# Weight conversions, unit steps and weight requests of a fused attention and mixer kernel moved in their order

## Chip, cores and metric

The kernel runs on one core of one Trainium2 chip. The metric is device time of one execution in microseconds. The core has five engines with queues of their own: TensorE (PE, matrix products), VectorE (DVE), ScalarE (ACT), GpSimd (POOL) and SyncE (SP, which here issues most transfers). Each runs its instructions in a fixed order and waits, at an instruction, until what that needs is done.

## The reference

Three stages follow one another for 4 sequences of 448 tokens, in float32: causal attention of 12 heads of 64, a mixer (tokens, then channels), and a second mixer with rotations.

```
scores = q @ k.T / 8, causal mask; attn = softmax(scores); x = attn @ v   # 4 x 12 heads, 448 x 64
u  = x + (relu(x.T @ w_tok1) @ w_tok2).T          # 448 -> 256 -> 448 tokens
x  = u + relu(u @ w_ch1) @ w_ch2                  # 768 -> 1536 -> 768 channels
theta = x @ w_theta
y  = w_tok_r @ (x * cos(theta)) + w_tok_i @ (x * sin(theta))
u  = x + y
out = u + relu(u @ w_ch)
```

The weights arrive as float64.

## The kernel before

**Pairs and steps.** Attention runs over 24 pairs of heads (6 in each sequence), each in 7 tiles of queries: 168 *steps*. A step's scores are one product on PE (line 273, for pairs from the ninth on with a second product at 275 for the low part of k). DVE masks them and finds the row maximum (L280), ACT takes the exponential (L282). For the first twelve pairs PE then transposes the result (L289), ACT copies it (L291) and PE multiplies it with v (L317). From the 13th pair on ACT writes a 16-bit high part `ph` (L110), DVE a low part (L302), SP issues a DMA that transposes both (`pt`, L305), and PE multiplies with v split in three (L328; DVE makes the splits `v_mid`). The product with v comes four steps behind its score (`LAG`). After every second pair `tokmix` does the token mixer for these heads.

**Units.** The channel mixer is cut into 96 *units*, 24 for each sequence: 12 weight tiles of `w_ch1` (`ch1_unit`) and 12 of `w_ch2` (`ch2_unit`), each 18 products on PE (L169 to L171: values and weights are split in a high and a low part) with one weight tile of 768 KB in `ws`, and one or two sums on ACT and DVE (L385, L386, L394). Units of a sequence that is done run between the steps of the next ones. `UNIT_STEPS` says at which step each runs: the first at step 46, 18 in the first 42 steps, then 26 in every 42. Units that are left run behind the last step.

**Conversions.** A weight tile is fetched as raw 64-bit words (L123), made float32 by one operation of ACT (L126) and four of DVE (L133 to L137), and split by ACT (L110) and DVE (L117) into `ws`. All 24 tiles of the channel mixer are converted during attention, and stored for the later sequences (`w_c<-ws`, L445). `ROUND_STEPS` says at which step each conversion starts: the first four are the token mixer's, four tiles of the channel mixer (`EARLY`) at steps 20 to 38 are stored and read again for the first sequence's units (L164), the other 20 start five steps ahead of their unit, which takes the tile directly from the conversion. `ws` has four buffers.

**Requests.** `run_units` asks, ahead of each unit, for the weight tiles of this and the next two units (`load_unit`), if they are stored. SP issues all of these transfers, in order, with the loads of q, k and v and the transposes.

**Order.** Within this the order of each engine's instructions is set when the program is built, by a scheduler with priorities (scores, their products with v and the loads of pairs come first) and a model of its own. So a table of steps also moves instructions that it doesn't name.

Of the kernel before, what the change touches and what calls it, by code (L numbers as in the profile page):

```python
# [21 lines left out]
NPR = H // 2  # L22
# [9 lines left out]
AHEAD, LAG, LOOK = 500, 4, 2  # L32
KEEP, UBACK = 6, 16
LATE_CONVERT = 16
FIRST_UNIT, PHASE, RATES = 46, 42, (18, 26)
EARLY = 4
UNIT_STEPS = [FIRST_UNIT + -(-n * PHASE // RATES[0]) if n < RATES[0] else
              FIRST_UNIT + PHASE + -(-(n - RATES[0]) * PHASE // RATES[1]) for n in range(72)]
ROUND_STEPS = [3, 4, 8, 9] + [20, 26, 32, 38] + [UNIT_STEPS[n] - 5 for n in range(EARLY, 24)]
ENGINES = {  # L40
    0: dict(qhi="A", qlo="D", khi="A", klo="D", v="D", phi="A", xhi="A", xlo="D", uhi="A", ulo="D"),
}
# [10 lines left out]
def fused(ctx, tc, q, k, v, w_tok1, w_tok2, w_ch1, w_ch2, w_theta, w_tok, w_ch, out):  # L53
# [15 lines left out]
    nc = tc.nc  # L69
# [29 lines left out]
    def hl_tile(tag):  # L99
        return main.tile([P, 2, S], F32R, tag=tag, name=tag, bufs=BUFS[tag])  # L100
# [4 lines left out]
    def f32v(ap):  # L105
        return ap.bitcast(F32)

    def copy_to(eng, dst, src, scale=1.0):
        if eng == "A":
            nc.scalar.activation(dst, src, AF.Copy, scale=scale)  # L110
        else:
            e = nc.gpsimd if eng == "P" else nc.vector
            e.tensor_scalar(out=dst, in0=src, scalar1=scale, scalar2=0.0, op0=ALU.mult, op1=ALU.add)  # L113

    def rest_to(eng, dst, src, hi):
        e = nc.gpsimd if eng == "P" else nc.vector
        e.tensor_tensor(out=dst, in0=src, in1=f32v(hi) if hi.dtype == F32R else hi, op=ALU.subtract)  # L117

    def raw_tile():
        return cv.tile([P, E, 2], U32, tag="raw", name="raw", bufs=BUFS["raw"])  # L120

    def fetch64(src, raw):
        nc.sync.dma_start(out=raw[:, :src.shape[-1]].rearrange("p n w -> p (n w)"), in_=src.bitcast(U32))  # L123
# [18 lines left out]
    def split_w(dst, f):  # L142
        copy_to("A", dst[:, 0], f)
        rest_to("D", dst[:, 1], f, dst[:, 0])
# [6 lines left out]
    def ws_tile():  # L151
        return main.tile([P, 2, E], F32R, tag="ws", name="ws", bufs=BUFS["ws"])
# [9 lines left out]
    def stream_tile(kept):  # L162
        w = ws_tile()
        nc.sync.dma_start(out=f32v(w), in_=kept)  # L164
        return w
# [29 lines left out]
    def tok_weights(n):  # L195
        if n < 2:
            cols = slice(n * 512, (n + 1) * 512)
            return w_tok1[:, cols], wt1[:, :, cols]
        return w_tok2[:, (n - 2) * S:(n - 1) * S], wt2[:, n - 2]
# [9 lines left out]
    def prep(b, pr):  # L209
        qr = ap2.tile([P, 2 * S], F32, tag="qk_raw", name="q_raw", bufs=2)  # L210
        if b * NPR + pr in NATIVE:
            kr = ap2.tile([P, 2 * S], F32, tag="kh", name="k_pad")
            for t, src in ((kr, k), (qr, q)):
                (nc.vector if b * NPR + pr == 0 and t is kr else nc.gpsimd).memset(t[64:128], 0.0)
                if b * NPR + pr == 0 and t is qr:
                    for c in (slice(0, 2 * P), slice(2 * P, 2 * S)):
                        nc.scalar.dma_start(out=t[0:64, c], in_=src[b, pr, 0:64, c])
                else:
                    loads[b * NPR + pr] = nc.sync.dma_start(out=t[0:64], in_=src[b, pr, 0:64])
        else:  # L220
            loads[b * NPR + pr] = nc.sync.dma_start(out=qr, in_=q[b, pr])
            kr = ap2.tile([P, 2 * S], F32, tag="qk_raw", name="k_raw", bufs=2)
            nc.sync.dma_start(out=kr, in_=k[b, pr])
        vr = ap2.tile([P, 9 * D], F32, tag="v_raw", name="v_raw")
        nc.sync.dma_start(out=vr, in_=v[b, pr])
        if b * NPR + pr in NATIVE:
            qs, kh, kl = qr, kr, None
        else:
            qs = ap2.tile([P, 2 * S], F32R, tag="qs", name="qs")
            copy_to(pick("qhi"), qs, qr)  # L230
            rest_to(pick("qlo"), qs[64:128], qr[64:128], qs[64:128])
            kh = ap2.tile([P, 2 * S], F32R, tag="kh", name="kh")
            copy_to(pick("khi"), kh, kr)
            kl = ap2.tile([P, 2 * S], F32R, tag="kl", name="kl")
            rest_to(pick("klo"), kl, kr, kh)
        if b * NPR + pr in NATPV:
            return qs, kh, kl, (vr,)
        v1 = vr.bitcast(BF16).rearrange("p (n w) -> p n w", w=2)[:, :, 1]
        vm = ap2.tile([P, 9 * D], F32, tag="v_mid", name="v_mid", bufs=1)
        rest_to(pick("v"), vm, vr, v1)  # L240
        v2, v3 = (vm.bitcast(BF16).rearrange("p (n w) -> p n w", w=2)[:, :, z] for z in (1, 0))
        rest_to(pick("v"), v3, vm, v2)
        return qs, kh, kl, (v1, v2, v3)
# [157 lines left out]
    loaded = {}  # L401

    jobs = [((w_ch1, w_ch2)[c - 1][fh * 6 + t], wd[f"c{c}", fh, t]) for _, fh, c, t in units[:24]]
    late = [(w_ch[e], wd["c3", 0, e]) for e in range(DT)]

    def load_unit(n):
        if n < len(units) and n not in loaded and (n >= 24 or n in stored):
            b, fh, c, t = units[n]
            loaded[n] = stream_tile(wd[f"c{c}", fh, t])

    fetched, rounding, stored = {}, {}, set()
    at, halves = [0], [0]

    def split_ready():

        while halves[0] < B * DT:
            b, d = divmod(halves[0], DT)
            if accs[b][d] is None or (d >= BUFS["ut"] - DT and at[0] < 24 * (b - 1) + 18):
                return
            t = hl_tile("ut")  # L420
            copy_to(pick("uhi"), t[:, 0], accs[b][d])
            rest_to(pick("ulo"), t[:, 1], accs[b][d], t[:, 0])
            uTs[b][d] = t
            halves[0] += 1

    def fetch(j):
        if j < len(ROUND_STEPS):
            src = tok_weights(j)[0] if j < 4 else jobs[j - 4][0]
            fetched[j] = src, raw_tile()
            fetch64(*fetched[j])  # L430

# [3 lines left out]
        abs64(rounding[j], raw)  # L435

    def round_rest(j):
        f = rounding.pop(j)
        round64(f, fetched.pop(j)[1])
        if j < 4:  # L440
            split_w(tok_weights(j)[1], f)
        else:
            w, kept = ws_tile(), jobs[j - 4][1]
            split_w(w, f)
            nc.sync.dma_start(out=kept, in_=f32v(w))  # L445
            stored.add(j - 4)
            if j - 4 >= EARLY:
                loaded[j - 4] = w
        fetch(j + 2)

    made = [0]
# [7 lines left out]
    def run_units(n):  # L459
        for _ in range(n):  # L460
            u = at[0]
            for ahead in range(LOOK + 1):
                load_unit(u + ahead)
            b, fh, c, t = units[u]
            if c == 1:
                ch1_unit(b, uTs[b], fh, t, loaded[u])
            else:
                ch2_unit(b, uTs[b], accs[b], fh, t, loaded[u])
            loaded[u] = None
            at[0] += 1  # L470
            split_ready()


# [2 lines left out]
    def pick(what):  # L476
        turn[what] = turn.get(what, -1) + 1
        return eng[what][turn[what] % len(eng[what])]
# [17 lines left out]
    for n, (b, pr, t) in enumerate(steps):  # L496
        if t == 0:
            eng.update(ENGINES.get(b * NPR + pr, {}))
        if t == 0:
            pairs[b, pr] = Pair(b, pr, parts[b, pr])  # L500
        with tc.high_priority(AHEAD):
            scores(pairs[b, pr], *TILES[t])
        if n == 0:
            fetch(0)
            fetch(1)
        for j, at_step in enumerate(ROUND_STEPS):
            if at_step == n - 1:
                with tc.issue_after(pairs[b, pr].first.ins):
                    round_rest(j)
            if at_step == n:  # L510
                with tc.issue_after(pairs[b, pr].last.ins):
                    round_first(j)
        if n >= 140:
            convert_late((n - 136) // 4)
        if t == 0 and (b, pr) != (B - 1, NPR - 1):
            nx = (b + (pr + 1) // NPR, (pr + 1) % NPR)
            with tc.high_priority(AHEAD), ExitStack() as es:
                if nx == (0, 1):
                    es.enter_context(tc.issue_after(loads[0].ins))
                parts[nx] = prep(*nx)  # L520
        if n >= LAG:
            with tc.high_priority(AHEAD):
                late_step(n - LAG)
        if n == FIRST_UNIT - 4:
            load_unit(0)
            load_unit(1)
        run_units(sum(at_step == n for at_step in UNIT_STEPS))
    for n in range(len(steps) - LAG, len(steps)):
        late_step(n)
# [111 lines left out]
    for b in range(B):  # L641
        raw, x2 = [], []
        for d in range(DT):
            r = acc_tile()
            nc.sync.dma_start(out=r, in_=x2d[b][d])
            t = hl_tile("ut")
# [126 lines left out]
```

## Time and profile before

| | us |
|---|---|
| three timed runs | 936.09, 937.81, 940.9 |
| median | 937.81 |
| profiled execution | 935.52 |
| its span, first to last instruction | 933.7 |
| PE busy | 903.5 |
| DVE busy | 633.0 |

The profile is one execution. A span's time counts from its first instruction. A wait is put down to what came last by the record; where several things are waited for, the one named may not be the one that held. L and a number is the line of the kernel.

### The profile page before, as it was taken

The numbers are of one execution on the slowest core, as the hardware profiler recorded it, in microseconds if no ns is written. First come the engines' busy times: TensorE is split into PE (matmuls) and PEld (weight loads), VectorE is DVE, ScalarE is ACT, GpSimd is POOL, SyncE is SP. The second block draws the span as 40 slices with busy tenths as digits, with TensorE's granted clock in tenths as the row PEclk, the third lists the DMA queues.
The fourth block names the chain that finished last, engine by engine and source line by source line (L and its number), as shares of the span: only waits on it lengthen the run. The fifth ranks groups of instructions, "written<-read, shape, count | busy, mean of one in ns | idle before, by whom it ended". The sixth has DMA issues, their size and how long they took to land.

```text
span 933.7 us, 15879 instructions
## 1 busy us (share of the span) xinstructions
PE 903.5 (97%) x5820; PEld 827.0 (89%) x5820; DVE 633.0 (68%) x1467; ACT 389.5 (42%) x914; POOL 109.5 (12%) x178
## 2 busy tenths in 40 slices
PE   7999999999879999999999999999999999999998
PEld 5888898988758899989989899999999999999997
DVE  5687798989997667667873398745764467475351
ACT  5777667667655545544632234312211202112100
POOL 2110000000000000000000000022531143242120
PEclk9999999999999999999999999999999999999999
DMA  5475686869899999699798599764605135153043
GB/s 169 133 248 197 235 288 206 293 225 262 246 285 318 323 250 238 227 263 279 232 315 260 178 352 401 261 207 134 200 1 152 56 114 166 29 161 109 24 131 127
DMA packets 103677, 193.65 MB, mean 207 GB/s; under 512 B 60784, under 2 KB 72880, under 8 KB 103600
## 3 DMA queue, kind: packets, MB, share of 16 engines
q1 hardware_dynamic: 102288, 190.84, 65.0%
q0 software_dynamic: 1152, 1.57, 0.9%
q8 instruction: 46, 0.75, 0.3%
q10 hardware_dynamic: 160, 0.23, 0.1%
q14 instruction: 31, 0.25, 0.1%
HBM read 143.85 MB, written 34.60 MB: 191 GB/s over the span
## 4 chain that ended last, share of the span: by engine, by line
PE 75%; DMA 12%; DVE 8%; ACT 3%; issue 2%; POOL 0%; SPq 0%; ACTq 0%; POOLq 0%; DVEq 0%
PE ps_mm L169 17%; PE ps_mm L170 17%; PE ps_mm L171 17%; DMA pt<-ph 7%; PE ps_sc L273 3%; PE ps_pv L317 3%; PE ps_sc L170 3%; PE ps_sc L169 3%; PE ps_sc L171 3%; PE ps_pv L328 2%; DMA ws<-w_c 2%; PE ps_mm L289 2%; DMA raw<-in_w_ch_dram 1%; DMA q_raw<-in_q_dram 1%; PE ps_sc L275 1%
## 5 line engine op out<-in xcount | busy, mean ns | idle before, releaser
L171 PE MATMUL ps_mm<-h,ws 128*128 128x448 f32 x432 | 159.7, 370 | 1.0 <-DVE ws L117 1.0
L169 PE MATMUL ps_mm<-h,ws 128*128 128x448 f32 x432 | 159.9, 370 | 0.5 <-ACT ws L110 0.5
L170 PE MATMUL ps_mm<-h,ws 128*128 128x448 f32 x432 | 159.7, 370 | 0.0
L169 PE MATMUL ps_mm<-ut,ws 128*128 128x448 f32 x288 | 106.8, 371 | 1.7 <-DMA ws<-w_c 1.7
L170 PE MATMUL ps_mm<-ut,ws 128*128 128x448 f32 x288 | 105.9, 368 | 0.0
L171 PE MATMUL ps_mm<-ut,ws 128*128 128x448 f32 x288 | 105.7, 367 | 0.0
L282 ACT ACTIVATE sb<-sb,mx 128x192 f32<-128x192 f32 (+3 forms) x168 | 89.5, 534 | 38.9 <-DVE mx L280 38.4
L171 PEld LDWEIGHTS ps_mm<-h,ws 128*128 128x128 f32 x432 | 81.6, 189 | 8.8 <-DVE ws L117 1.7
L169 PEld LDWEIGHTS ps_mm<-h,ws 128*128 128x128 f32 x432 | 81.5, 189 | 8.1 <-ACT ws L110 0.7
L170 PEld LDWEIGHTS ps_mm<-h,ws 128*128 128x128 f32 x432 | 81.6, 189 | 6.9
L280 DVE CUSTOM_DVE_ANT_0 sb<-ps_sc,mask 128x192 f32<-128x192 f32 (+3 forms) x168 | 74.6, 454 | 15.2 <-PE ps_mm L289 11.1
L113 POOL TENSOR_SCALAR ut<-acc 128x448 fp32r<-128x448 f32 x24 | 17.2, 722 | 508.4 <-PE ps_mm L355 450.0
L577 ACT ACTIVATE tmp<-ps_sc 128x384 f32<-128x384 f32 x28 | 13.5, 483 | 132.2 <-PE ps_sc L171 132.1
L317 PEld LDWEIGHTS ps_pv<-v_raw,ptf 128*128 128x128 f32 x456 | 58.7, 191 | 6.3 <-ACT ptf L291 2.2
L317 PE MATMUL ps_pv<-v_raw,ptf 128*128 128x128 f32 (+1 forms) x456 | 62.6, 275 | 1.3 <-issue 0.6
L302 DVE SCALAR_TENSOR_TENSOR ph<-sb,ph 128x64 f16<-128x64 f32 (+3 forms) x156 | 42.9, 316 | 27.3 <-ACT ph L110 26.7
L169 PEld LDWEIGHTS ps_mm<-ut,ws 128*128 128x128 f32 x288 | 54.1, 188 | 6.1 <-DMA ws<-w_c 1.9
L110 ACT ACTIVATE ph<-sb 128x192 f16<-128x192 f32 (+3 forms) x84 | 36.8, 444 | 53.4 <-DMA pt<-ph 52.9
L170 PEld LDWEIGHTS ps_mm<-ut,ws 128*128 128x128 f32 x288 | 54.2, 188 | 4.4 <-issue 0.2
L171 PEld LDWEIGHTS ps_mm<-ut,ws 128*128 128x128 f32 x288 | 54.1, 188 | 4.2
L386 DVE SCALAR_TENSOR_TENSOR h<-ps_mm,h 128x448 fp32r<-128x448 f32 x48 | 29.7, 618 | 34.2 <-ACT h L385 34.0
L584 ACT ACTIVATE tmp<-tmp 128x384 f32<-128x384 f32 x28 | 14.7, 526 | 85.5 <-DVE tmp L582 85.5
(151 smaller groups left out, 2110.1 us busy)
## 6 DMA issues: line engine op xcount, KB each, us to landing
ws<-w_c SPq DMA_DIRECT2D x100, 768.0 KB, 5.7
raw<-in_w_ch_dram SPq DMA_DIRECT2D x30, 768.0 KB, 5.1
w_c<-ws SPq DMA_DIRECT2D x30, 768.0 KB, 4.7
q_raw<-in_q_dram SPq DMA_DIRECT2D x16, 448.0 KB, 4.2
k_raw<-in_k_dram SPq DMA_DIRECT2D x16, 448.0 KB, 4.7
v_raw<-in_v_dram SPq DMA_DIRECT2D x24, 288.0 KB, 4.1
x2d<-acc SPq DMA_DIRECT2D x24, 224.0 KB, 4.7
acc<-x2d SPq DMA_DIRECT2D x24, 224.0 KB, 3.2
```

The source lines that it names most:

```text
L110: nc.scalar.activation(dst, src, AF.Copy, scale=scale)
L169: nc.tensor.matmul(ps, lhsT=ka(a[:, 0]), rhs=kb(b[:, 0]), start=first, stop=False)
L170: nc.tensor.matmul(ps, lhsT=ka(a[:, 0]), rhs=kb(b[:, 1]), start=False, stop=False)
L171: nc.tensor.matmul(ps, lhsT=ka(a[:, 1]), rhs=kb(b[:, 0]), start=False, stop=last)
L273: nc.tensor.matmul(ps[:, 0:n], lhsT=lhs, rhs=cut(pp.kh), start=True, stop=pp.kl is None)
L280: pp.first = nc.vector.tensor_tensor_reduce(out=dst, in0=src, in1=msk, op0=ALU.add, op1=ALU.min, scale=-0.125, scalar=3.0e38, accum_out=pp ...
L282: pp.last = nc.scalar.activation(sb[:, 0:kk], sb[:, 0:kk], AF.Exp, bias=pp.mx[:, j:j + 1], scale=-1.0, accum_out=pp.sm[:, j:j + 1])
L289: nc.tensor.transpose(pst[:, u * P:(u + 1) * P], full[:, c0 + u * P:c0 + (u + 1) * P], ident)
L302: nc.vector.scalar_tensor_tensor(out=dst, in0=sb[:, c0:c1], scalar=PSC, in1=hi[:, c0:c1], op0=ALU.mult, op1=ALU.subtract)
L317: nc.tensor.matmul(pp.ps[:, reg:reg + n], lhsT=pt[:, u], rhs=pp.v[0][:, vt * D:vt * D + n], start=(u == 0), stop=(u == len(blks) - 1))
L328: nc.tensor.matmul(pp.ps[:, reg:reg + D], lhsT=pt[:, blk], rhs=pp.v[c][:, vt * D:(vt + 1) * D], start=(n == 0), stop=(n == len(jobs) - 1))
L386: gates[0] = nc.vector.scalar_tensor_tensor(out=t[:, 1], in0=ps[:, 0:S], scalar=0.0, in1=f32v(t[:, 0]), op0=ALU.max, op1=ALU.subtract)
```

## The change

`UNIT_STEPS` gets other rates: 14 units in the first 42 steps from 46 on, then 29 in every 42. The conversions get a table of their own: six tiles (0 to 5) four steps apart from step 18 on and five more (14, 16, 18, 20, 22) between steps 43 and 70 are converted ahead, stored, and read again; the other 13 start five steps ahead of their unit and are taken directly. Requests for weight tiles stand behind a unit: for the next two units for the first 24, for the next three after that. The clearing of the lower half of the first q tile goes from POOL to DVE.

```diff
-FIRST_UNIT, PHASE, RATES = 46, 42, (18, 26)
-EARLY = 4
+FIRST_UNIT, PHASE, RATES = 46, 42, (14, 29)
-ROUND_STEPS = [3, 4, 8, 9] + [20, 26, 32, 38] + [UNIT_STEPS[n] - 5 for n in range(EARLY, 24)]
+AHEAD_STEPS = {0: 18, 1: 22, 2: 26, 3: 30, 4: 34, 5: 38, 14: 43, 16: 47, 18: 51, 20: 55, 22: 70}
+ROUNDINGS = sorted([(at_step, n - 4) for n, at_step in enumerate((3, 4, 8, 9))] +
+                   [(AHEAD_STEPS.get(n, UNIT_STEPS[n] - 5), n) for n in range(24)])
...
-                (nc.vector if b * NPR + pr == 0 and t is kr else nc.gpsimd).memset(t[64:128], 0.0)
+                (nc.vector if b * NPR + pr == 0 else nc.gpsimd).memset(t[64:128], 0.0)
...
     def fetch(j):
-        if j < len(ROUND_STEPS):
-            src = tok_weights(j)[0] if j < 4 else jobs[j - 4][0]
+        if j < len(ROUNDINGS):
+            n = ROUNDINGS[j][1]
+            src = tok_weights(n + 4)[0] if n < 0 else jobs[n][0]
...
     def round_rest(j):
-        f = rounding.pop(j)
+        n, f = ROUNDINGS[j][1], rounding.pop(j)
         round64(f, fetched.pop(j)[1])
...
             nc.sync.dma_start(out=kept, in_=f32v(w))
-            stored.add(j - 4)
-            if j - 4 >= EARLY:
-                loaded[j - 4] = w
+            stored.add(n)
+            if n not in AHEAD_STEPS:
+                loaded[n] = w
...
             u = at[0]
-            for ahead in range(LOOK + 1):
-                load_unit(u + ahead)
+            load_unit(u)
...
             at[0] += 1
+            for ahead in range(LOOK + (u >= 24)):
+                load_unit(at[0] + ahead)
             split_ready()
```

In the changed program's rows line numbers are one to three higher behind the table.

POOL's order at the start of the program, before (`k_pad` and `q_raw` are the padded tiles of a pair's k and q, `sb` and `x` work tiles):

```order
L214 MEMSET k_pad 64x896
L178 MEMSET mask 128x448
masks.py:199 ISA
masks.py:199 AFFINE_SELECT ident<-ident 128x128
L191 MEMSET sb_148 128x64
L191 MEMSET sb_150 128x64
L191 MEMSET sb_152 128x64
L204 MEMSET x_154 128x128
L204 MEMSET x_156 128x128
L214 MEMSET q_raw 64x896 x2
L179 AFFINE_SELECT mask<-mask 128x128
```

and now:

```order
L215 MEMSET k_pad 64x896
L215 MEMSET q_raw 64x896
L179 MEMSET mask 128x448
masks.py:199 ISA
masks.py:199 AFFINE_SELECT ident<-ident 128x128
L192 MEMSET sb_148 128x64
L192 MEMSET sb_150 128x64
L192 MEMSET sb_152 128x64
L205 MEMSET x_154 128x128
L205 MEMSET x_156 128x128
L180 AFFINE_SELECT mask<-mask 128x128
```

Of the two clearings of `q_raw` that stood next to each other behind the work tiles, the first pair's has gone to DVE and the second pair's stands ahead of them.

DVE's order from the 96th score on, before (`ws` and `wf` are a conversion's tiles, `x` attention's result, L372 and L394 sums of tokmix and of a unit):

```order
L280 ISA sb_152,mx<-ps_sc,mask 128x320
L280 ISA mx 128x1
L117 TENSOR_TENSOR v_mid<-v_raw 128x576
L335 TENSOR_TENSOR x_154<-ps_pv,sm 128x384
L340 TENSOR_SCALAR x_154<-ps_pv,sm 64x64 x2
L117 TENSOR_TENSOR ws<-wf,ws 128x768
L137 SCALAR_TENSOR_TENSOR wf<-raw,wf 128x768
L280 ISA sb_148,mx<-ps_sc,mask 128x448
L280 ISA mx 128x1
L372 TENSOR_TENSOR acc<-ps_mm,acc 128x448 x2
L302 SCALAR_TENSOR_TENSOR ph<-sb_150,ph 128x64
L302 SCALAR_TENSOR_TENSOR ph<-sb_150,ph 128x256
```

and now:

```order
L281 ISA sb_152,mx<-ps_sc,mask 128x320
L281 ISA mx 128x1
L118 TENSOR_TENSOR v_mid<-v_raw 128x576
L336 TENSOR_TENSOR x_154<-ps_pv,sm 128x384
L341 TENSOR_SCALAR x_154<-ps_pv,sm 64x64 x2
L281 ISA sb_148,mx<-ps_sc,mask 128x448
L281 ISA mx 128x1
L118 TENSOR_TENSOR kl<-k_raw,kh 128x896
L281 ISA sb_150,mx<-ps_sc,mask 128x448
L281 ISA mx 128x1
L118 TENSOR_TENSOR qs<-q_raw,qs 64x896
L134 TENSOR_SCALAR wf<-wf 128x768
```

The two conversion operations between the 96th and the 97th score are gone from there, and the 98th score follows one operation behind the 97th.

SP's order around the first transposes, before (`raw` is a conversion's fetch, `w_c<-ws` its store, the numbers in `w_c` the tile):

```order
L223 DMA k_raw<-in_k_dram 128x896
L445 DMA w_c_1_4_103<-ws 128x1536
L305 DMA_TRANSPOSE pt<-ph 128x2x128
L123 DMA raw<-in_w_ch_dram 128x1536
L305 DMA_TRANSPOSE pt<-ph 128x3x128
L445 DMA w_c_1_5_104<-ws 128x1536
L225 DMA v_raw<-in_v_dram 128x576
L305 DMA_TRANSPOSE pt<-ph 128x3x128
L305 DMA_TRANSPOSE pt<-ph 128x5x128
```

and now:

```order
L224 DMA k_raw<-in_k_dram 128x896
L124 DMA raw<-in_w_ch_dram 128x1536
L165 DMA ws<-w_c_1_2_101 128x1536
L447 DMA w_c_1_1_100<-ws 128x1536
L306 DMA_TRANSPOSE pt<-ph 128x2x128
L306 DMA_TRANSPOSE pt<-ph 128x3x128 x2
L124 DMA raw<-in_w_ch_dram 128x1536
L165 DMA ws<-w_c_1_4_103 128x1536
L226 DMA v_raw<-in_v_dram 128x576
```

Two weight tiles of the first sequence (14 and 16) are now read back here, where before the conversions' stores and a fetch stood between the transposes.

## Rows read from the trace of the kernel before

**Rows 1.** Part 1 of the page: busy us (share of the span) and instructions.
```profile
PE 903.5 (97%) x5820; PEld 827.0 (89%) x5820; DVE 633.0 (68%) x1467; ACT 389.5 (42%) x914; POOL 109.5 (12%) x178
```

**Rows 2.** Busy time by stretch: length, PE, PEld, DVE, ACT, POOL, clock, DMA, GB/s.
```profile
0.00:77.30 77.30, 70.54 (x470) 60.02 (x471) 54.55 (x163) 54.29 (x151) 12.96 (x27) 1.00 0.57 172
77.30:204.50 127.20, 125.20 (x819) 115.35 (x818) 105.18 (x231) 85.74 (x196) 1.98 (x2) 1.00 0.72 250
204.50:307.50 103.00, 89.66 (x737) 80.80 (x736) 94.16 (x234) 64.18 (x150) 0.00 (x0) 0.98 0.94 282
307.50:470.90 163.40, 161.70 (x1346) 146.93 (x1344) 114.26 (x318) 83.24 (x204) 0.00 (x0) 1.00 0.91 256
...
528.00:933.70 405.70, 401.14 (x2073) 373.31 (x2071) 238.52 (x467) 85.29 (x182) 94.54 (x150) 1.00 0.47 154
```

**Rows 3.** The same view: 26 us within the third stretch, and 20 of products alone.
```profile
256.00:282.00 26.00, 19.32 (x184) 16.02 (x182) 25.46 (x66) 15.05 (x38) 0.00 (x0) 0.93 0.95 269
...
560.00:580.00 20.00, 20.00 (x101) 18.46 (x100) 15.86 (x40) 8.77 (x21) 0.83 (x1) 1.00 1.03 407
```

**Rows 4.** Waits of PE, 204.5 to 307.5: us in total, times, longest.
```profile
PE ps_pv L328 <- DMA pt<-ph: 8.6, 6, 2.1
PE ps_mm L169 <- DMA ws<-w_c: 1.7, 1, 1.7
PE ps_pv L328 <- issue: 1.2, 1, 1.2
```

**Rows 5.** DVE's groups, 204.5 to 307.5: busy us, mean ns, idle before.
```profile
L137 DVE SCALAR_TENSOR_TENSOR wf<-raw,wf 128x768 uint32<-128x768 uint32 x9 | 8.6, 954 | 0.0
L136 DVE SCALAR_TENSOR_TENSOR wf<-raw,wf 128x768 uint32<-128x768 uint32 x9 | 8.6, 953 | 0.0
L117 DVE TENSOR_TENSOR ws<-wf,ws 128x768 fp32r<-128x768 f32 x8 | 7.7, 958 | 0.1
...
L133 DVE TENSOR_SCALAR wf<-wf 128x768 f32<-128x768 f32 x9 | 5.0, 556 | 0.8 <-ACT wf L126 0.8
L134 DVE TENSOR_SCALAR wf<-wf 128x768 uint32<-128x768 uint32 x9 | 5.0, 555 | 0.0
...
L386 DVE SCALAR_TENSOR_TENSOR h<-ps_mm,h 128x448 fp32r<-128x448 f32 x7 | 4.3, 621 | 0.6 <-ACT h L385 0.6
...
L394 DVE TENSOR_TENSOR acc<-ps_mm,acc 128x448 f32<-128x448 f32 x6 | 3.7, 611 | 0.0
L302 DVE SCALAR_TENSOR_TENSOR ph<-sb,ph 128x256 f16<-128x256 f32 x8 | 3.4, 423 | 0.0
...
L117 DVE TENSOR_TENSOR v_mid<-v_mid 128x576 bf16<-128x576 f32 x4 | 3.3, 831 | 0.0
```

**Rows 6.** Instructions in order of time, the first 6 us: start, us, what.
```profile
0.76 1.46 SPq L219 DMA_DIRECT2D k_pad<-in_k_dram  x2
...
3.32 1.63 POOL L214 MEMSET q_raw<- 64x896 f32 x2
...
5.07 1.41 PE L273 MATMUL ps_sc<-k_pad,q_raw 128*128 128x128 f32 x4 [5.07 <-POOL q_raw L214]
```

**Rows 7.** Transfers issued in the first 0.9 us: KB each, us to landing.
```profile
k_pad<-in_k_dram SPq DMA_DIRECT2D x1, 224.0 KB, 4.2
```

**Rows 8.** Transfers issued from 204.5 to 307.5; last, tiles in ws alone.
```profile
ws<-w_c SPq DMA_DIRECT2D x6, 768.0 KB, 6.9
...
pt<-ph SPq DMA_TRANSPOSE x28, 4.8
...
DMA to landing us min/median/max: 3.2/6.0/9.5
```

**Rows 9.** Waits of SP, 204.5 to 307.5: us in total, times, longest.
```profile
SPq L305 <- DVE ph L302: 10.8, 10, 2.7
...
SPq L445 <- DVE ws L117: 5.4, 3, 3.7
```

More of the change, by code (lines that the diff above doesn't have):

```diff
@@ L437, in round_rest @@
     def round_rest(j):
-        f = rounding.pop(j)
+        n, f = ROUNDINGS[j][1], rounding.pop(j)
         round64(f, fetched.pop(j)[1])
-        if j < 4:
-            split_w(tok_weights(j)[1], f)
+        if n < 0:
+            split_w(tok_weights(n + 4)[1], f)
         else:
-            w, kept = ws_tile(), jobs[j - 4][1]
+            w, kept = ws_tile(), jobs[n][1]
             split_w(w, f)
             nc.sync.dma_start(out=kept, in_=f32v(w))
-            stored.add(j - 4)
-            if j - 4 >= EARLY:
-                loaded[j - 4] = w
+            stored.add(n)
+            if n not in AHEAD_STEPS:
+                loaded[n] = w
         fetch(j + 2)
@@ L505, in fused @@
             fetch(1)
-        for j, at_step in enumerate(ROUND_STEPS):
+        for j, (at_step, _) in enumerate(ROUNDINGS):
             if at_step == n - 1:
```

## Prediction

> **What bounds the kernel now.** I started from the busy shares of the whole execution. TensorE (PE) is busy 903.5 of 933.7 us, VectorE (DVE) 633.0 [rows 1]. So nothing but about 30 us of PE idle time, and what hides inside busy time, can be won by any reordering, for the matrix products are the same before and after. Then I read busy time by stretch, cut at PE's 43rd, 85th and 117th score product (scores of a step: one of 168) [rows 2]. The reader is to see where the idle time sits. From 77.3 to 204.5 us PE is busy 125.20 of 127.20. From 204.5 to 307.5 it is busy 89.66 of 103.00: 13.3 us idle, more than in any other stretch. In this one stretch DVE is busy 94.16 us, 91%; in the 26 us from 256 it is 25.46, 98%, with PE at 19.32 [rows 2, 3]. From 307.5 on PE is again busy 161.70 of 163.40.
>
> The waits in that stretch name DMA: PE's second product of attention waits 8.6 us in six waits for transposed probabilities (pt) [rows 4]. But a transpose lands in 4.8 us at the median [rows 8], and SyncE (SP), which issues it, waits itself: 10.8 us in ten waits for DVE's low part of the probabilities [rows 9]. So the chain is score, DVE, ScalarE, DVE, SP, DMA, PE, and the engine that is full in it is DVE. What fills DVE is above all five operations for each converted weight tile, 954, 953, 958, 556 and 555 ns, 3.98 us a tile [rows 5], some nine times in this stretch, 35 us of the 94.
>
> One more place: PE starts at 5.07 us behind GpSimd's (POOL) clearing of q_raw, issued at 3.32 for 1.63 [rows 6]. The same score waits for k_pad, whose transfer is issued at 0.76 and lands 4.2 us later, at 4.96 [rows 6, 7].
>
> **The change part by part.** *Clearing q_raw on DVE.* POOL's end at 4.95 goes, k_pad's landing at 4.96 stays. Gain 0.0 to 0.1 us; I take 0. DVE's extra clearing stands ahead of its first score and is hidden: DVE has 54.55 us of work in 77.3 [rows 2].
>
> *Conversions.* Counted in the order of the two programs between DVE's 85th and 117th score, the DVE operations of conversions go from 42 to 34: one fewer at each of lines 133 and 134, two fewer at 136, 137 and 117 (ws). That is 0.556 + 0.555 + 2 x 0.953 + 2 x 0.954 + 2 x 0.958 = 6.8 us [rows 5]. Against it stand one more operation at each of lines 386 and 394 (0.62 + 0.61) and one more v_mid split with two fewer at line 302 (0.83 less 2 x 0.42, nothing). DVE's load in the stretch becomes 94.2 - 6.8 + 1.2 = 88.6 us. The work comes back ahead of score 43: nine operations more, 2 x 0.556 + 2 x 0.555 + 0.953 + 2 x 0.954 + 2 x 0.958 = 7.0 us, on 54.55 of 77.3, so DVE stands at 80% there. PE waited 6.8 us there with 54.55, most of it the start; I price what may be added with the tighter stretch below.
>
> *Units, 14 and 10.* A unit is 18 products. A stretch of such products has 101 in 20.00 us, 0.198 us each [rows 3]. Between PE's 43rd and 85th score the unit products go from 253 to 207, -46; up to the 117th from 233 to 260, +27; behind it +19. In stretches where PE is full this is time: -9.1 us from 77.3 to 204.5, +3.8 us behind 307.5. In between 27 x 0.198 = 5.3 us of PE work go into a stretch that has 13.3 us of holes. This is the main term: DVE sets that stretch's length, and PE's work in it is free up to the holes.
>
> *How long that stretch is then.* From PE: 89.66 + 5.3 = 95.0 us of busy time. From DVE: 88.6 us; at the share of now (91%) that is 97 us, at the 97% of its first 77.5 us 92. The upper end is that the holes stay: 103.0 + 5.3 = 108.3. The lower end is PE full, and the clock too: the granted clock of the 26 us from 256 is 0.93, so 3.6 us at 1.2 GHz instead of 2.4, after PE had been idle in the waits for pt [rows 3, 4]; that cost 1.8 us, and 95.0 - 1.8 = 93.2. I take 97, where the nearest row, DVE's share of the same stretch, puts it, and PE's own bound lies 2 us below.
>
> Weight loads are busy 80.80 us in this stretch, and 18.46 of 20.00 where PE is full [rows 2, 3]. The Trainium skill (Perfetto Trace Analysis, "Identifying the Most-Contended Engine") says that matmul busy time is no good measure of how near TensorE is to its limit, and that the busy share of weight loads is; by that rule the stretch holds 80.80 / 0.923 = 87.5 us of work in place of 89.66, 92.8 with the new units, and the lower end would be 0.4 us lower. The trace leans to it, since the half clock stands in matmul busy time.
>
> *The tighter stretch before.* From 77.3 to 204.5 DVE keeps nearly its load (105.18 less 2.8 by the same counting: three unit operations, and little of the conversions) while the stretch loses 9.1 us: 87% of 118 us instead of 83%. It also has one heap: between DVE's 77th and 78th score now stand two tiles' worth of conversions and the sums of tokmix, some 14 us. There PE can wait. Bounds: nothing, or the share of idle time that the full stretch shows now, 13% of some 35 us, 4.5 us. I take 2 us for this and the start together.
>
> *Weights that come back from memory.* Eleven instead of four tiles of the first batch are stored and read again. Reads in the stretch land in 6.9 us at the median [rows 8]. They are asked for behind a unit for the unit after next, some 2.9 steps of 3.2 us (103.0 / 32), 9.3 us ahead. Covered at the median; 0 now, the worst is a rival. For units from the 25th on the new place of the request names the same three tiles one unit boundary earlier, 0.
>
> *Sum.* Stretch 77.3 to 204.5: -9.1. Stretch to 307.5: 103.0 to 97, -6.0. Behind: +3.8. New waits: +2. Together -9.3 us. The profiled execution took 935.52 us (span 933.7); so 926.2 in its terms. The three timed runs have a median of 937.81 (936.09 to 940.9), 2.3 above the profiled one; on their scale 928.5.
>
> **The rivals.** *Holes filled, clock kept.* PE becomes the bound of the stretch, 93.2 us, and no new wait comes: -9.1 - 9.8 + 3.8 = -15.1, 922.7. For it: DVE's 88.6 us lie below PE's 93. Against: from a score to the landing of its transpose is a chain of five hand-overs, and DVE's order is fixed in heaps.
>
> *The holes only move.* The heap ahead of DVE's 78th score and the fuller stretch before it cost as much as the full stretch gives back. Four and a half us there, 2 at the start, and a stretch of 100 in place of 97 give -9.1 - 3.0 + 3.8 + 6.5 = -1.8, 936. For it: eight of 42 conversion operations is a small relief. Against: PE idled only 2.0 us at 83% DVE [rows 2].
>
> *Late weights, slower.* In the stretch the DMA engines are 94% busy [rows 2]; SP is held by a store up to 3.7 us [rows 9], and the slowest tile took 9.5 to land [rows 8], 13.2 together against 9.3 of notice. Then a reloaded unit stops PE for up to 3.9 us, and the scores queued behind it on PE too. The five tiles 14, 16, 18, 20 and 22 alone make 5 x 3.9 = 19.5 us, -9.3 + 19.5 = +10, 948. It decides from a mean lateness of 1.9 us on. Against: six such reads in this stretch now cost PE one wait of 1.7 us [rows 4, 8], and conversions fetch fewer raw tiles there.
>
> **How the numbers follow.** Forecast 928.5, with 0.50, its own range 923 to 934 (2 us of each of the two uncertain terms, the stretch's 97 and the new waits' 2, and a run's spread of 2). Filled holes 0.17 at 922.7; moved holes 0.20 at 936; late weights 0.13 at 948. The range reaches to the moved holes with a run's spread, 940, and down to 919, and leaves out the late weights and little else. About 0.5%, 4.7 us, is what a measurement of this kernel can tell from no change: faster is below 933.1. That holds for the filled holes, for 0.47 of the forecast's 0.50 and for 0.01 of the moved ones: 0.65. Within: 0.03, 0.18 of the moved and 0.02 of the late weights: 0.23. Slower: 0.12.
>
> **What would show it.** Right: the stretch from PE's 85th to 117th score lasts 95 to 99 us, PE busy over 96% of it, DVE near 88 us; the 85th score comes near 195 us, the 117th near 292; PE's wait for transposed probabilities falls from 8.6 us to under 4; PE still starts at 5.0. Wrong: the 85th score comes later than 200 us (heap before it), the stretch lasts over 103 us (DVE's chain is not the bound), or PE waits for weight reads more than 4 us in all (late weights). A start before 4.5 us would show that k_pad did not hold PE.

## The result, and the profile after

The changed kernel took 928.39 us (median of four runs, 925.48 to 930.39), the kernel before, on the same chip, 936.95 (the three timed runs and a fourth of 935.7): a ratio of 0.989, with a 95% interval of 0.9867 to 0.9913. The forecast was 928.5.

The profiled execution took 928.29 us with a span of 926.5, against 935.52 and 933.7. First part 1 of the page: busy us, share of the span, instructions.

```profile
PE 903.3 (97%) x5820; PEld 828.8 (89%) x5820; DVE 633.5 (68%) x1468; ACT 387.5 (42%) x914; POOL 108.6 (12%) x177
```

PE is busy as long as before, 903.3 against 903.5 us [rows 1]. So of the 7.2 us by which the span is shorter 7.0 are idle time of PE: 30.2 us before, 23.2 now. Where it went is in the busy time by stretch, cut at the same scores as in [rows 2] (the 43rd falls at 76.7 us, the 85th at 196.1, the 117th at 293.0):

```profile
0.00:76.70 76.70, 69.60 (x469) 59.61 (x470) 60.93 (x170) 56.85 (x152) 12.44 (x26) 1.00 0.62 196
76.70:196.10 119.40, 116.25 (x770) 108.85 (x769) 104.57 (x231) 85.60 (x199) 1.62 (x2) 0.99 0.82 290
196.10:293.00 96.90, 94.26 (x764) 86.70 (x763) 88.48 (x224) 58.53 (x139) 0.00 (x0) 0.96 0.99 291
293.00:926.50 633.50, 623.19 (x3826) 573.65 (x3822) 379.50 (x845) 186.55 (x426) 94.58 (x150) 1.00 0.62 191
```

The third row is the one to read. PE idled 13.3 us of this stretch before and now idles 2.6; it is busy 97% of the stretch. The four stretches changed by -0.6, -7.8, -6.1 and +7.3 us. Next, all waits of PE over the whole span (us in total, times, longest):

```profile
PE ps_sc L274 <- DMA k_pad<-in_k_dram: 5.0, 1, 5.0
PE ps_mm L354 <- ACT xg L111: 2.6, 2, 1.8
PE ps_pv L329 <- DMA pt<-ph: 2.3, 3, 1.3
PE ps_sc L274 <- DVE mx L281: 1.9, 4, 0.6
PE ps_mm L355 <- DVE xg L118: 1.9, 1, 1.9
PE ps_pv L329 <- issue: 1.9, 1, 1.9
...
PE ps_mm L170 <- DMA ws<-w_c: 0.4, 1, 0.4
```

The 8.6 us for `pt` of [rows 4] are 2.3 now; the 1.7 for weights read back are 0.4. DVE's conversion operations between 196.1 and 293.0 us, to be laid beside [rows 5] (busy us, mean ns, idle before):

```profile
L138 DVE SCALAR_TENSOR_TENSOR wf<-raw,wf 128x768 uint32<-128x768 uint32 x8 | 7.7, 958 | 0.1
L137 DVE SCALAR_TENSOR_TENSOR wf<-raw,wf 128x768 uint32<-128x768 uint32 x8 | 7.6, 954 | 0.0
L118 DVE TENSOR_TENSOR ws<-wf,ws 128x768 fp32r<-128x768 f32 x6 | 5.7, 957 | 0.3 <-ACT ws L111 0.2
...
L134 DVE TENSOR_SCALAR wf<-wf 128x768 f32<-128x768 f32 x7 | 3.9, 558 | 0.0
L135 DVE TENSOR_SCALAR wf<-wf 128x768 uint32<-128x768 uint32 x7 | 3.9, 552 | 0.0
```

28.8 us in place of the 34.9 that [rows 5] add up to: 6.1 us gone, of the same durations. And the transfers issued in this stretch, with the median us to landing, to be laid beside [rows 8]:

```profile
ws<-w_c SPq DMA_DIRECT2D x10, 768.0 KB, 7.3
...
pt<-ph SPq DMA_TRANSPOSE x27, 5.1
```

Both are a little slower than before (6.9 and 4.8), and PE waits for neither as it did. So the time that a transpose takes was not what PE's old waits were about. That it came late because its input did is tested by light_before below.

### The profile page after: what moved, and what is told of

Read it like the earlier page. It is cut to its first block, busy times and chain, and to the rows that moved or that the text cites. A ratio compares the mean times of both kernels' runs of the same rounds, so it can differ in the third digit from the quotient of the medians.

```text
span 926.5 us, 15932 instructions
## 1 busy us (share of the span) xinstructions
PE 903.3 (97%) x5820; PEld 828.8 (89%) x5820; DVE 633.5 (68%) x1468; ACT 387.5 (42%) x914; POOL 108.6 (12%) x177
## 4 chain that ended last, share of the span: by engine, by line
PE 80%; DMA 10%; DVE 5%; ACT 3%; issue 1%; SPq 1%; ACTq 0%; DVEq 0%
PE ps_mm L172 17%; PE ps_mm L170 17%; PE ps_mm L171 17%; DMA pt<-ph 9%; PE ps_pv L318 4%; PE ps_sc L274 3%; PE ps_sc L172 3%; PE ps_sc L170 3%; PE ps_sc L171 3%; PE ps_mm L290 2%; PE ps_pv L329 2%; PE ps_mm L354 1%; PE ps_mm L355 1%; PE ps_mm L356 1%; DMA raw<-in_w_tok_dram 1%
## 5 line engine op out<-in xcount | busy, mean ns | idle before, releaser
L386 ACT ACTIVATE h<-ps_mm 128x448 fp32r<-128x448 f32 x48 | 25.9, 539 | 59.9 <-PE ps_mm L172 59.9
## 6 DMA issues: line engine op xcount, KB each, us to landing
v_raw<-in_v_dram SPq DMA_DIRECT2D x24, 288.0 KB, 4.9
```

Of the source, the lines that this page charges most:

```text
L386: nc.scalar.activation(t[:, 0], ps[:, 0:S], AF.Relu)
```

## The experiments

The theory was the prediction's: DVE's load sets the length of the dense stretch (85th to 117th score), and the change gains what PE had idled there. Medians below stand beside a median of the kernel before on the same chip.

**The new unit rates alone.** The kernel before with one line changed:

```diff
-FIRST_UNIT, PHASE, RATES = 46, 42, (18, 26)
+FIRST_UNIT, PHASE, RATES = 46, 42, (14, 29)
```

> The kernel before with the unit rates 14 and 29 and nothing else; its conversions stay five steps ahead of their units, so they slide into the dense stretch with them. Counted in the order of this program between the 85th and 117th score: 60 DVE operations of conversions in place of 42 (47.7 us in place of 33.7), 196 unit products in place of 233; 53 products fewer ahead of it, 90 more behind. Theory (DVE's load sets this stretch): DVE has 94.2 + 14.0 = 108 us there, the stretch lasts 108 to 113 us although PE has 7.3 us less to do in it; in all -10.5 + 8 + 17.8 = +15, about 952 us. Rival (the later units make the gain, the table of conversions is of no account): 928 to 932 us. Rival (SP's transposes set the stretch): with 7.3 us less PE work in it about 101 to 103 us, +7, 944 us.

Measured: 949.26 us (945.18 to 953.82) beside 936.93, ratio 1.0117 (1.0089 to 1.0145). Busy time by stretch:

```profile
191.00:240.00 49.00, 45.55 (x359) 41.71 (x358) 47.86 (x117) 34.36 (x78) 0.00 (x0) 0.97 0.86 258
240.00:300.00 60.00, 44.10 (x296) 37.98 (x296) 51.40 (x121) 29.56 (x64) 0.00 (x0) 0.80 0.93 248
```

The total is what the theory gave within 3 us. The first rival is out; the second's 944 lies only 1.2 us below the fastest run, and light_before decides on it. The place was misjudged, by the theory's 108 to 113 us and by the second rival's 101 to 103: by PE's scores the stretch lasts 97.0 us, since PE issued its 117th score at 288.0 and went on with units and tokmix until DVE took the score up, 27 us later, with 14 more operations of conversions ahead of it; by DVE's own scores it is 196.8 to 315.2, 118 us. In the first row DVE is busy 98%, in both together PE idles 19.4 us of 109. PE's waits from 191 to 300 us show the links of the chain that [rows 4] and [rows 9] had shown:

```profile
PE ps_pv L328 <- DMA pt<-ph: 7.3, 3, 4.0
PE ps_sc L273 <- DVE mx L280: 4.9, 4, 1.9
PE ps_mm L169 <- ACT ws L110: 3.0, 2, 2.4
...
```

**The table of conversions alone.** The changed kernel with the old rates:

```diff
-FIRST_UNIT, PHASE, RATES = 46, 42, (14, 29)
+FIRST_UNIT, PHASE, RATES = 46, 42, (18, 26)
```

> The changed kernel with the old unit rates 18 and 26: only the table of conversions, the requests and the clearing are new. Between the 85th and 117th score 26 DVE operations of conversions in place of 42 (20.8 us in place of 33.7) and, as the order comes out, 291 unit products in place of 233; 6 products more ahead, 64 fewer behind. Theory (DVE's load sets the stretch): DVE has about 84 us there, PE 89.7 + 58 x 0.198 = 101 us and is the bound, the stretch lasts 101 to 104 us; +1.2 + 0 - 12.7 + 2 of waits ahead, where DVE has 6 us more: about 927 us (924 to 931), the whole gain without the new rates. Rival (the rates make the gain): 935 to 938 us. Rival (heaps ahead of the 85th score cost what is won): the 85th score comes after 209 us, 935 us or more.

Measured: 929.12 us (927.33 to 932.53) beside 936.93, ratio 0.9913 (0.9886 to 0.9939). The stretches from the 43rd, from the 85th and from the 117th score:

```profile
76.80:204.80 128.00, 125.81 (x824) 116.81 (x823) 113.33 (x242) 89.70 (x204) 1.53 (x2) 1.00 0.87 307
204.80:307.70 102.90, 100.06 (x794) 90.72 (x793) 83.49 (x219) 59.17 (x145) 0.00 (x0) 0.98 0.94 277
307.70:927.00 619.30, 605.04 (x3743) 557.49 (x3738) 376.94 (x837) 182.90 (x417) 95.09 (x150) 1.00 0.61 188
```

This has the gain of the whole change without the rates, as far as the two intervals tell (0.9867 to 0.9913 for the change). The dense stretch is as long as before, but PE is busy 100.06 us of it in place of 89.66: 291 unit products stand in it, 58 more, and 64 fewer behind. The scheduler pulled the units forward as soon as DVE left room. Not all of it arrives: behind the 117th score PE has 13.1 us less to do than before, but idles 14.3 us there in place of 8.1. And DVE at 89% from 76.8 to 204.8 us costs PE only 2.2 us there.

**DVE's load taken out of the kernel before.** In the last nine conversions three of four operations are skipped:

```diff
-        nc.vector.tensor_scalar(out=f, in0=f, scalar1=W64_MIN, ...
+        if not light:
+            nc.vector.tensor_scalar(out=f, in0=f, scalar1=W64_MIN, ...
...
-        round64(f, fetched.pop(j)[1])
+        round64(f, fetched.pop(j)[1], j - 4 >= 15)
```

> The kernel before, but the conversions of the last nine tiles (those that start from step 76 on) leave out three of their four DVE operations behind ScalarE's (lines 133, 134 and 136; the tiles' values are then not the weights): 2.07 us less DVE work a tile, 18.6 us in all. The order follows: between the 85th and 117th score 21 conversion operations in place of 42, 311 unit products in place of 233, 77 fewer behind. Theory (DVE's load sets the stretch): PE's idle time in it falls from 13.3 us to under 4, PE is busy over 96% of it, and the total falls by 9 to 11 us, 926 to 928. Rival (the way through SP and the transposing DMA, or the weight reads, sets it): PE keeps 9 to 13 us of idle time there and the total stays at 934 to 938.

Measured: 924.3 us (923.18 to 926.55) beside 936.93, ratio 0.9855 (0.983 to 0.988). The dense stretch:

```profile
204.20:307.70 103.50, 102.05 (x803) 92.82 (x802) 82.80 (x212) 64.01 (x150) 0.00 (x0) 1.00 1.03 309
```

PE's idle time falls from 13.3 to 1.5 us, with the tables of unit steps and conversions, the requests and the transposes as before and with more traffic (309 GB/s against 282); 311 unit products stand in it, 78 more. DVE's load did set this stretch; the way through SP and the DMA engines did not. The 12.6 us are more than the 9 to 11 expected; the two profiled executions differ by 9.0 (924.7 against 933.7), so the rest may be scatter between runs.

**The same in the changed kernel.**

```diff
-        round64(f, fetched.pop(j)[1])
+        round64(f, fetched.pop(j)[1], ROUNDINGS[j][0] >= 77)
```

> The changed kernel, its conversions from step 77 on (seven tiles) without the same three DVE operations (lines 134, 135 and 137; the tiles' values are then not the weights): 14.5 us less DVE work. Between the 85th and 117th score the order has 18 conversion operations in place of 34. Theory (with the change PE is the bound of this stretch, DVE no longer): PE's idle time there can fall by no more than its 2.6 us, and what the half clock cost; 924 to 928 us in place of 928.4. Rival (DVE still sets the stretch): it shortens by 6 us or more, 922 or less.

Measured: 927.89 us (925.35 to 930.67) beside 937.78, ratio 0.9892 (0.9867 to 0.9917). The stretch:

```profile
193.00:283.40 90.40, 89.17 (x741) 81.08 (x740) 78.85 (x208) 59.42 (x143) 0.00 (x0) 1.00 1.08 314
```

The stretch is 6.5 us shorter, which the rival had asked for, but the total is not: the stretch holds 12 unit products fewer (2.4 us), which run later, PE idles 1.2 us in it in place of 2.6, and its granted clock is 1.00 in place of 0.96. By the totals, which decide, 14.5 us less of DVE work bring nothing that these runs can tell (0.9867 to 0.9917, and 0.9867 to 0.9913 for the change itself), where 18.6 had brought 12.6. DVE no longer bounds the kernel here.

**Requests ahead of the unit again.**

```diff
-            load_unit(u)
+            for ahead in range(LOOK + 1):
+                load_unit(u + ahead)
...
-            for ahead in range(LOOK + (u >= 24)):
-                load_unit(at[0] + ahead)
```

> The changed kernel with the requests for weight tiles ahead of the unit again, for this and the next two. Unit products and conversions stand in the same stretches as in the changed kernel. Theory: reads of stored tiles have 9 us of notice and land in 7, so neither place costs PE anything: 928 us within 2, PE's waits for ws under 1 us. Rival (the later request frees SP's queue for transposes): SP is held longer by ws reads that wait for a buffer, PE's waits for pt grow by 3 us or more, 932 us or more. Rival (the later request made tiles late): faster by 2 us or more.

Measured: 928.96 us (925.58 to 931.38) beside 936.93, ratio 0.9896 (0.9871 to 0.9921). PE waits 1.4 us for `pt` and shows no wait for `ws` reads. The place of the request is worth nothing that these runs can tell.

**The heap at the 77th score.** In the changed kernel PE waits 1.9 us for tokmix's low part `xg`, and 1.4 us later its products turn slow. Its products there in order of time (start, us, what, in brackets the idle time before):

```profile
171.30 0.49 PE L354 MATMUL ps_mm<-xg,wt 128*128 128x256 f32 x2
...
174.19 0.39 PE L355 MATMUL ps_mm<-xg,wt 128*128 128x256 f32 x1 [1.90 <-DVE xg L118]
174.42 0.28 PE L356 MATMUL ps_mm<-xg,wt 128*128 128x256 f32 x1
...
176.13 0.41 PE L355 MATMUL ps_mm<-xg,wt 128*128 128x256 f32 x1
```

Busy time by stretch shows the granted clock of these moments; 0.53 is nearly all at the lower of its two levels, 1.2 GHz in place of 2.4, which is called the half clock here:

```profile
174.00:175.60 1.60, 1.41 (x12) 1.41 (x13) 1.60 (x6) 0.63 (x2) 0.00 (x0) 1.00 1.02 416
175.60:179.20 3.60, 3.60 (x19) 3.51 (x18) 3.60 (x7) 1.10 (x4) 0.00 (x0) 0.53 1.00 365
```

DVE's instructions in order of time, from just before PE begins to wait:

```profile
171.72 0.95 DVE L118 TENSOR_TENSOR ws<-wf,ws 128x768 fp32r<-128x768 f32 x1
172.59 0.95 DVE L137 SCALAR_TENSOR_TENSOR wf<-raw,wf 128x768 uint32<-128x768 uint32 x1
173.45 0.69 DVE L118 TENSOR_TENSOR xg<-x,xg 128x512 fp32r<-128x512 f32 x1
```

Two operations of two different conversions stand ahead of `xg`. One line spreads them:

```diff
-AHEAD_STEPS = {..., 14: 43, 16: 47, 18: 51, 20: 55, 22: 70}
+AHEAD_STEPS = {..., 14: 42, 16: 46, 18: 50, 20: 53, 22: 56}
```

> The changed kernel with the five stored tiles 14, 16, 18, 20, 22 at steps 42, 46, 50, 53, 56 in place of 43, 47, 51, 55, 70, so that no two conversions start within two steps around the 77th score. Theory (the heap of two conversions between DVE's 77th and 78th score makes PE's wait for xg there, 1.9 us, and the half clock behind it): both go, PE's time above its usual interval in 160 to 180 us falls from 3.5 to under 1; 925 us (923 to 927). Rival (the sums of the token mixer alone make that wait): 928 us, the wait stays. Rival (the earlier conversions crowd the stretch before the 43rd score and the heap comes back there): PE waits 2 us or more for mx or xg ahead of the 60th score, 928 us or more.

Measured: 926.52 us (921.88 to 928.26) beside 937.78, ratio 0.9881 (0.9856 to 0.9907). PE has no wait at all from 160 to 190 us, and the products of that tokmix go through at the full rate (start, us, what):

```profile
171.59 0.28 PE L355 MATMUL ps_mm<-xg,wt 128*128 128x256 f32 x1
171.71 0.28 PE L356 MATMUL ps_mm<-xg,wt 128*128 128x256 f32 x1
171.83 0.28 PE L354 MATMUL ps_mm<-xg,wt 128*128 128x256 f32 x1
```

So the heap made the wait. But at the next tokmix PE now waits longer than it did: 2.7 us for `xg` between 190 and 232 us, against 0.8 in the changed kernel between 196 and 225. Whether the 2 to 3 us that the heap costs reach the total was tried once more, with both kernels on one chip:

> The changed kernel itself, once more, beside the next one on one chip: 928 us within 1.5, its wait for xg behind the 77th score again near 1.9 us with some 3 us of half clock behind it.

> The kernel three_apart once more, on the same chip as the changed kernel. Theory (the heap at the 77th score costs the changed kernel its wait and the half clock behind it): 1.5 to 3.5 us faster than the changed kernel beside it. Rival (the 1.9 us between the two seen so far, on different chips and with overlapping intervals, are scatter): within 1 us of it.

Measured: 929.19 us (925.11 to 930.25) for the changed kernel, with the wait of 1.9 us and the slow products behind it again, and 927.39 (925.35 to 930.37) for three_apart. The medians differ by 1.9 and 1.8 us in the two comparisons, but single runs of one kernel spread over 5 us or more, and the intervals against before overlap (0.9865 to 0.9925 and 0.985 to 0.9911). That the wait goes is shown; that the kernel is faster for it is likely and not shown.

**Rates in between.** three_apart with

```diff
-FIRST_UNIT, PHASE, RATES = 46, 42, (14, 29)
+FIRST_UNIT, PHASE, RATES = 46, 42, (16, 28)
```

> The kernel three_apart with unit rates 16 and 28 in place of 14 and 29. Between the 85th and 117th score 294 unit products in place of 259, 31 conversion operations in place of 35. Theory (once DVE does not bound the dense stretch, the place of a unit is free, since PE's work is the same): as three_apart within 2 us, 925. Rival (later units are worth something of their own): 3 us or more slower than three_apart. Rival (units between the two rates fill holes that both leave): 3 us or more faster.

Measured: 926.52 us (923.49 to 927.47) beside 937.78, ratio 0.9873 (0.9848 to 0.9897): the median of three_apart to the digit, which is chance within runs that spread over 4 us. Within what these runs can tell, where a unit stands is free once DVE is not full.

**One step more for the probabilities.**

```diff
-AHEAD, LAG, LOOK = 500, 4, 2
+AHEAD, LAG, LOOK = 500, 5, 2
-BUFS = dict(..., ph=3, pt=5)
+BUFS = dict(..., ph=3, pt=6)
```

> The changed kernel with the product with v five steps behind its score in place of four, and six pt buffers in place of five. Theory (what PE still waits for from 196 us on is the way of the probabilities through DVE, SP and the transposing DMA, some 9 us at four steps): PE's waits for pt, 2.3 us and 1.9 more before its first such product, fall under 1 us, and the half clock behind the second of them, 6.8 us long, goes; -4 to -6, 922.5 to 925 us. Rival (what is waited for then is the token mixer, which comes a step later too): waits for xg grow as those for pt fall, 927 to 930 us. Rival (the new order makes heaps elsewhere): 930 or more.

Measured: 927.94 us (925.77 to 928.81) beside 937.78, ratio 0.9888 (0.9864 to 0.9912). Its waits of PE over the span:

```profile
PE ps_pv L329 <- DMA pt<-ph: 6.4, 5, 2.3
...
PE ps_mm L354 <- ACT xg L111: 2.1, 2, 1.8
...
PE ps_mm L355 <- DVE xg L118: 0.3, 1, 0.3
```

Its dense stretch:

```profile
193.90:294.50 100.60, 98.02 (x773) 89.45 (x772) 90.08 (x224) 60.66 (x143) 0.00 (x0) 1.00 1.02 307
```

A miss of the theory: the half clock in the dense stretch did go (1.00 in place of 0.96), but the waits for `pt` grew from 2.3 us (4.2 with the 1.9 that PE waited ahead of its first such product) to 6.4 with a step more of time, and those for `xg` fell instead. The time is that of the changed kernel. Why a later product should meet later transposes was not followed further.

## Why the prediction was right, and where it was not

**What bounded the kernel.** Right, and shown: DVE's load in the dense stretch. Its relief alone brings 12.6 us (light_before), and no change to requests or transposes was needed for it; with more conversions in the stretch the kernel takes 12.3 us longer (units_alone).

**The start.** Right: no gain that can be told. PE starts at 4.96 us in place of 5.07 [rows 6]. In units_alone POOL still clears `q_raw` behind its work tiles, and PE starts at 4.79, held by the landing of `k_pad`:

```profile
3.32 1.63 POOL L214 MEMSET q_raw<- 64x896 f32 x2
...
4.79 2.05 PE L273 MATMUL ps_sc<-k_pad,q_raw 128*128 128x128 f32 x6 [4.79 <-DMA k_pad<-in_k_dram]
```

**Conversions.** Right in size: the forecast of 88.6 us for DVE's load in the stretch met 88.48; in the first 76.7 us it rose by 6.4 (7.0 forecast).

**The dense stretch.** 96.9 us for a forecast of 97, with the 85th score at 196.1 (near 195) and the 117th at 293.0 (near 292). The number rested on DVE's share of 91% staying, and it is 91.3%. But that share did not set the length: PE's 2.6 us of idle time lie ahead of 225 us, and behind that PE is full while DVE stays at 91%:

```profile
225.00:260.00 35.00, 35.00 (x281) 31.66 (x280) 31.92 (x81) 22.32 (x54) 0.00 (x0) 1.00 0.96 281
260.00:293.00 33.00, 33.00 (x290) 30.20 (x289) 29.99 (x78) 17.76 (x43) 0.00 (x0) 1.00 1.06 317
```

light_after says the same. PE's own busy time, 94.26 us for 95.0 forecast, with the idle time, gives 97 as well. The two limits lie so close that a right number cannot tell them apart; that DVE's share named it was luck.

Weight loads, the other measure that the prediction weighed, were busy 80.80 of 103.00 us before and are 86.70 of 96.90 now. Read against the 92.3% of a stretch where PE is full [rows 3], that leaves 3.0 us free (96.90 less 86.70 / 0.923), and PE idled 2.6. The Trainium skill (Perfetto Trace Analysis, "Identifying the Most-Contended Engine") says to judge TensorE by this share and not by matmul busy time; the trace agrees here. The reason for which the prediction leaned to it, that the half clock stands in matmul busy time, does not hold: it stands in weight loads too. In the kernel before the granted clock is 0.51 from 265.0 to 268.5 us and 1.00 behind that:

```profile
265.00:268.50 3.50, 3.50 (x11) 3.14 (x10) 3.47 (x6) 0.29 (x1) 0.00 (x0) 0.51 1.08 194
268.50:282.00 13.50, 10.36 (x118) 8.71 (x117) 13.04 (x37) 8.65 (x23) 0.00 (x0) 1.00 0.98 319
```

A weight load takes 0.33 us in the first of these rows and 0.19 in the second (start, us, what):

```profile
265.63 0.33 PEld L170 LDWEIGHTS ps_mm<-h,ws 128*128 128x128 f32 x1
...
268.95 0.19 PEld L171 LDWEIGHTS ps_mm<-h,ws 128*128 128x128 f32 x1
```

**The units.** This is the step that failed. The prediction called the new rates "the main term" and booked -9.1, +5.3 into holes and +3.8. As bookkeeping it holds: the recorded unit products are 207, 260 and 1693 for 253, 233 and 1674. As a cause it does not: the table of conversions without the rates has the gain (conversions_alone), and rates in between change nothing that these runs can tell. Moving a unit came out as a sum of zero for PE; room in DVE turned holes into work, and the scheduler found the work by itself. The rates alone make the kernel 12.3 us slower, for the conversions slid along with the units, 60 of their operations in the stretch in place of 42 (as the theory of units_alone had it), which the prediction never priced because it took the two tables together.

**The smaller terms.** New waits were taken as 2 us: from 76.7 to 196.1 us PE idles 3.2 in place of 2.0 [rows 2], the heap at the 77th score alone 1.9 of it; with them the two stretches to the 117th score came out as booked, -7.8 and -6.1 us for -7.1 and -6.0. Late weights were taken as 0 and are 0.4. The miss sits behind them. What comes there was forecast as +3.8 and is +7.3, 5.1 us of it busy (623.19 us against the 618.1 that [rows 1, 2] leave behind 307.5 us) and 2.2 idle, all three waits for `pt` of the list above among it; why the busy part is 1.3 us above the 19 moved products was not tried. In one execution against another the sum is -7.2 for a forecast of -9.3; between the medians of the result it is -8.6. The forecast of 928.5 on the scale of the runs is thus right partly by luck, because the median of before that it was added to lay 2.3 us above its profile.

**The rivals.** None came as it was priced. Of the filled holes the mechanism came in good part: PE is the bound of most of the stretch. Their number did not, 96.9 us for 93.2, for PE still idles 2.6 us and the clock was not kept (0.96). The heap of the moved holes is there, but it costs 1.9 us of waiting and some 3 us at half clock. Against late reads stand the 0.4 us of waiting and requests_ahead.

## What to carry to other kernels

Read the engine that is full in the stretch where the critical engine idles, not in the whole: DVE had 68% of the span and 91% of that stretch. The Trainium skill (Perfetto Trace Analysis, "Optimization Strategy") says that kernels can have regimes with different most-contended engines, and that interleaving them may help. Here 13.3 us of PE idle time went to 2.6 when a sixth of the conversion work in that stretch was done before it. When a change has two tables, price each alone: here the one that moved the full engine's work made the gain, and the one that moved work of the critical engine only shifted it about.

## What the runs showed of the hardware

A hole can cost more than its length. Behind the 1.9 us wait at 172 us PE's products in the changed kernel go from 0.28 to 0.41 us each for some 3 us, at a granted clock of 0.53, nearly all of it the half clock. Not every hole does: in the dense stretch before PE idled 13.3 us, and the granted clock was still 0.98 [rows 2]. In units_alone, where PE idles 19.4 us between 191 and 300, the granted clock from 240 to 300 us is 0.80, and PE is busy 915.35 us in all with the products that take 903.5 before: of the 18.3 us that its span is longer, 11.9 are busy time. The mean granted clocks account for that: 0.984 over 952.0 us leaves 15.2 us of full clock out, 0.996 over 933.7 leaves out 3.7, which is 11.5 us less.

A high busy share of the DMA engines was no sign of a bound: 0.94 in the dense stretch before, with PE idling 13.3 us [rows 2], and 1.03 to 1.08 in light_before and light_after, with PE busy 98.6%.
